# Attention, MoE and gated MLP on one core: cross-partition maxima on TensorE, a list schedule searched over 40 passes, and another way to put float64 weights together

## The chip, the cores and the metric

One Trainium2 chip, one of its cores. The time is that of one execution on the device in microseconds (us), as the median of several runs.

## What is computed

Three stages follow one another on 2304 rows (4 batches of 576 pooled queries, 8 heads of 64):

```python
q_pool = q.reshape(B, H, S // 2, 2, D).mean(axis=3)          # B, H, S, D = 4, 8, 1152, 64
scores = (1 / sqrt(D)) * q_pool @ k.transpose(0, 1, 3, 2)
attn = softmax(scores)                                        # over 1152 keys
x = heads side by side of (attn @ v)                          # 2304 x 512
h = x @ w_in;  x = (h * sigmoid(h)) @ w_out                   # 512 -> 2048 -> 512
out = (((x @ w1) * (x @ w2)) @ w3) @ w_out2                   # 512 -> 1024 -> 1024 -> 512
```

q, k and v are float32. The weights come as float64 and are read as pairs of 32-bit words.

## The kernel before

**Numbers.** Most products use float16 in two parts, a high one and a rest ("hi" and "lo"), each scaled by a power of two that comes from the largest absolute value of the tensor, so that three matmuls (`TERMS`) give nearly float32. Such a scale needs a maximum over all 128 partitions: VectorE (DVE) reduces along the row, `allmax` (L309) then takes the maximum over the partitions on GpSimd (POOL) and gives it to each of them, and `pow2` (L301) makes the scales in a few VectorE instructions on one column.

**Attention.** The work is 144 score tiles of 128 queries x 1152 keys. `tile_ops` (L446) makes, for each: scores on TensorE (PE) into one of two PSUM buffers `sc` (L465), the negative row maximum on VectorE (L502), the exponential with its row sum on ScalarE (ACT, L482), the reciprocal (L487, L490). For batch 0 (`WHOLE`, 36 tiles) the tile is then transposed in float32 on TensorE (L514) and copied out by ScalarE (L517); the reciprocals are spread by `dg` (L523) and a small matmul (`spread`, L562). For the other batches ScalarE and VectorE write a hi and a lo part (L530, L493) and a DMA transposes them (L498). `pv_ops` (L585) multiplies with v (L555 float32, L610 float16); ScalarE writes the result into `x32` (L620). `prep_v` (L386) makes v's two parts for batches 1 to 3, with its maximum (L401, L310).

**First MoE.** Its 9 blocks of 256 rows are made by `block_ops` (L626) and lie between the score tiles on the engines' queues: maximum of `x32` (L632), over partitions (L310), scales (L303 to L638), `x16` hi on ScalarE (L656) and lo on VectorE (L643), then 8 units of `w_in` products (L676), tanh and gate (L692, L695), the hi and lo part of g on ScalarE and GpSimd (L698, L701), 16 units of `w_out` products (L717) and the store.

**Weights.** `from_f64` (L312) makes float32 of the words: ScalarE moves the exponent (L324), then VectorE puts sign, exponent and fraction together in three instructions per 128x512 tile (L328 shifts left by 3, L329 brings in the top three bits of the low word, L330 the sign). There are 72 such tiles: 32 for the first MoE in the first 190 us, 40 for the last stage.

**Last stage.** `w3 @ w_out2` is multiplied out first (L1015), then blocks of 384 rows go through w1 and w2 (L1119), their product (L1139, L1145, L1150) and the final matmul (L1163). Each block's maximum goes over L1087 and L310.

**Order.** Every step is an `op` with an engine, a cost, the buffers that it reads and writes and a key. `Plan.run` (L115) is a list scheduler: engine by engine it takes, among the steps that could start within 0.15 us, the one of least key, and so fixes each engine's order, the order of the DMA issues on SP and which buffer a step gets. Each engine's queue runs in that order; semaphores are waited for in it.

Of the kernel before, what the change touches and what calls it, by code (L numbers as in the profile page):

```python
# [9 lines left out]
F32 = mybir.dt.float32  # L10
F32R = mybir.dt.float32r
F16 = mybir.dt.float16
I32 = mybir.dt.int32
AF = mybir.ActivationFunctionType
# [5 lines left out]
P = 128  # L20
# [7 lines left out]
LOAD_AFTER = 3.0  # L28
AFTER = {PE: 0.25, ACT: 0.2, DVE: 0.15, POOL: 0.2, SP: 0.0}
# [28 lines left out]
class Op:  # L58
    __slots__ = (
        "eng", "cost", "land", "fn", "key", "after", "need", "ready", "start", "end", "takes", "bufs", "n", "hook",  # L60
        "placed",
# [3 lines left out]
class Plan:  # L65
# [5 lines left out]
    def op(self, eng, cost, fn, r=(), w=(), key=0.0, land=None):  # L71
# [3 lines left out]
        o.n, o.hook = len(self.ops), None  # L75
# [39 lines left out]
    def run(self):  # L115
        cand = defaultdict(list)
        free = {e: 0.0 for e in ENGINES}
        free["CTL"] = 0.0
        order = []
# [17 lines left out]
        while any(cand.values()):  # L137
# [11 lines left out]
            assert best is not None, [o.n for some in cand.values() for o in some][:20]  # L149
            at, e, o = best  # L150
            cand[e].remove(o)
            o.start = at
            if e != "CTL":
                free[e] = at + o.cost
            o.end = at + (o.cost if o.land is None else o.land)
# [3 lines left out]
            for buf in o.takes:  # L159
                tag = buf.tag  # L160
                buf.place = min(tag.free, key=lambda s: (tag.free[s], s))
                del tag.free[buf.place]
                tag.next += 1
            for buf in o.bufs:
                buf.left -= 1
                buf.end = max(buf.end, o.end + AFTER.get(e, 0.0))
                if buf.left == 0:
                    buf.tag.free[buf.place] = buf.end
            for x in o.after:
# [15 lines left out]
def kernel(  # L185
# [51 lines left out]
    ident_b = Buf(Tag(1))  # L237

# [24 lines left out]
    t_sm = tags(attn, "sm", 8, [P, 4])  # L263
    t_mv = tags(attn, "mv", 6, [P, 5])
    t_rs = tags(attn, "rs", 1, [P, BL])
    t_dg = tags(attn, "dg", 4, [P, D])
# [42 lines left out]
    def allmax(dst, src):  # L309
        nc.gpsimd.partition_all_reduce(dst, src, channels=P, reduce_op=bass_isa.ReduceOp.max)  # L310

    def from_f64(dst, words, dst_b, words_b, key):  # L312
# [8 lines left out]

        def rebias():
# [9 lines left out]
        op(ACT, 0.68, rebias, [words_b], [dst_b], key)  # L332
        op(DVE, 1.85, merge, [words_b], [dst_b], key + 0.01)
# [13 lines left out]

    kts, qts, v16s, mvs = {}, {}, {}, {}
# [14 lines left out]
    def prep_q(b, g, hp):  # L363
# [20 lines left out]
        op(DVE, 0.7 + 0.13 * g, pool, [qs], [qt], i0 - 7)  # L384

    def prep_v(b, hp):  # L386
        i0 = FIRST_T[(b, 0, hp)]
        v16, mv = attn_buf(t_v16), attn_buf(t_mv) if b >= WHOLE else None
# [10 lines left out]

        def top():  # L400
            nc.vector.reduce_max(mv.t[:, 0:1], vs.t, axis=AX.X, apply_absolute_value=True)  # L401

        def scales():
            pow2(mv.t[:, 1:2], mv.t[:, 2:3], mv.t[:, 3:4])
            nc.vector.tensor_scalar_mul(mv.t[:, 3:4], mv.t[:, 3:4], 2.0 ** 13)
            nc.vector.tensor_scalar_mul(mv.t[:, 4:5], mv.t[:, 2:3], 2.0 ** -29)

        def hi():
            d_, s_ = parts()
            nc.scalar.activation(d_[:, :, 0, :], s_, AF.Copy, scale=mv.t[:, 3:4])  # L410

        def lo():
            d_, s_ = parts()
            nc.vector.scalar_tensor_tensor(
                d_[:, :, 1, :], s_, mv.t[:, 3:4], d_[:, :, 0, :], op0=ALU.mult, op1=ALU.subtract
# [14 lines left out]
        op(DVE, 1.36, top, [vs], [(mv, 0)], i0 - 4)  # L430
        op(POOL, 0.4, lambda: allmax(mv.t[:, 1:2], mv.t[:, 0:1]), [(mv, 0)], [(mv, 1)], i0 - 3.9)
        op(DVE, 0.8, scales, [(mv, 1)], [(mv, 2)], i0 - 2)
        op(ACT, 1.26, hi, [vs, (mv, 2)], [(v16, 0)], i0 - 1)
        op(DVE, 1.45, lo, [vs, (mv, 2), (v16, 0)], [(v16, 1)], i0 + 0.5)

    WHOLE = 1
    pts = {}
    x32s = {}  # L440
    dgs = {}

# [799 lines left out]
```

## Time and profile before

| | |
|---|---|
| median of 3 runs | 1200.62 us (1199.74 to 1205.22) |
| the profiled execution | 1200.74 us, span 1198.7 us |
| mean granted TensorE clock | 0.974 |
| TensorE busy | 1108.2 us (92%) |
| VectorE busy | 792.2 us (66%) |
| ScalarE busy | 663.2 us (55%) |
| GpSimd busy | 158.1 us (13%) |
| 16 DMA engines, hardware queue | 55.6% of the span |

TensorE's busy share is that of a whole span with stages of different limits, and a matmul at the lower clock counts as busy for longer (the nine transposes of one tile took 1.20 us in some places and 2.18 us in others). So the table is only a start: what a stage waits for is read from its own stretch, from the waits that TensorE ends last there, and from the granted clock beside them.

### The profile page before, as it was taken

The numbers are of one execution on the slowest core, as the hardware profiler recorded it, in microseconds if no ns is written. First come the engines' busy times: TensorE is split into PE (matmuls) and PEld (weight loads), VectorE is DVE, ScalarE is ACT, GpSimd is POOL, SyncE is SP. The second block draws the span as 40 slices with busy tenths as digits, with TensorE's granted clock in tenths as the row PEclk, the third lists the DMA queues.
The fourth block names the chain that finished last, engine by engine and source line by source line (L and its number), as shares of the span: only waits on it lengthen the run. The fifth ranks groups of instructions, "written<-read, shape, count | busy, mean of one in ns | idle before, by whom it ended". The sixth has DMA issues, their size and how long they took to land.

```text
span 1198.7 us, 21922 instructions
## 1 busy us (share of the span) xinstructions
PE 1108.2 (92%) x8972; PEld 809.1 (67%) x8972; DVE 792.2 (66%) x1283; ACT 663.2 (55%) x986; POOL 158.1 (13%) x156
## 2 busy tenths in 40 slices
PE   3778897999999999999899999897999999999998
PEld 2445675767776767677677777786756776767666
DVE  6988898498788788797987785576977521212110
ACT  3656667567677577686686675465634322222221
POOL 0000120012012012020020020112121111111211
PEclk9978998999999999999999999898999999999999
DMA  9635344368988997989979778454334001010001
GB/s 348 211 134 184 115 140 157 115 136 169 181 182 171 218 194 166 190 174 200 199 145 200 151 123 148 147 194 137 124 123 150 1 27 54 12 42 27 10 18 27
DMA packets 294821, 163.17 MB, mean 136 GB/s; under 512 B 256064, under 2 KB 266816, under 8 KB 294720
## 3 DMA queue, kind: packets, MB, share of 16 engines
q1 hardware_dynamic: 294720, 161.77, 55.6%
q8 instruction: 70, 1.15, 0.4%
q14 instruction: 31, 0.25, 0.1%
HBM read 80.22 MB, written 9.44 MB: 75 GB/s over the span
## 4 chain that ended last, share of the span: by engine, by line
PE 51%; DVE 3%; issue 2%; DMA 1%; ACT 1%; POOL 1%; DVEq 0%; POOLq 0%; ACTq 0%
PE mt L1119 10%; PE mm L676 7%; PE mt L1163 6%; PE mm L717 5%; PE sc L465 5%; PE mm L1119 4%; PE mm L610 4%; PE mt L1015 3%; PE mt L676 3%; PE mt L717 2%; PE mm L1163 2%; DMA pt<-p 1%; PE mm L1015 0%; DVE sm L502 0%; DVE x L643 0%
## 5 line engine op out<-in xcount | busy, mean ns | idle before, releaser
L465 PE MATMUL sc<-kt,qt 64*128 64x128 f32 (+3 forms) x960 | 200.7, 534 | 29.0 <-ACT pt L517 20.9
L502 DVE TENSOR_REDUCE sm<-sc 128x1 f32<-128x1152 f32 x144 | 193.9, 1348 | 40.5 <-PE sc L465 40.2
L676 PEld LDWEIGHTS <-w 128*128 128x128 f16 x1728 | 169.7, 100 | 60.6 <-issue 35.9
L482 ACT ACTIVATE e<-sc,sm 128x1152 f32<-128x1152 f32 x144 | 175.2, 1217 | 47.9 <-DVE sm L502 42.8
L717 PEld LDWEIGHTS <-w 128*128 128x128 f16 x1728 | 164.3, 98 | 54.2 <-issue 30.9
L676 PE MATMUL mm<-x,w 128*128 128x256 f16 x1440 | 173.2, 279 | 18.6 <-DVE x L643 9.7
L493 DVE SCALAR_TENSOR_TENSOR p<-e,sm,p 128x1152 f16<-128x1152 f32 x108 | 159.5, 1484 | 29.7 <-ACT p L530 29.2
L717 PE MATMUL mm<-g,w 128*128 128x256 f16 x1440 | 169.8, 273 | 2.8 <-POOL g L701 1.9
L465 PEld LDWEIGHTS sc<-kt,qt 64*128 64x128 f32 (+1 forms) x960 | 91.8, 182 | 97.9 <-issue 57.1
L530 ACT ACTIVATE p<-e,sm 128x1152 f16<-128x1152 f32 x108 | 134.2, 1248 | 31.4 <-DMA pt<-p 10.7
L701 POOL TENSOR_TENSOR g<-t,g 128x512 f16<-128x512 f32 x72 | 94.6, 1319 | 297.8 <-ACT g L698 237.0
L1139 DVE SCALAR_TENSOR_TENSOR abf<-mt,x2m,asb 128x384 f32<-128x384 f32 x36 | 22.1, 615 | 123.9 <-PE mt L1119 123.9
L610 PE MATMUL mm<-pt,v 128*64 128x256 f16 (+1 forms) x1944 | 89.8, 250 | 5.3 <-DMA pt<-p 5.1
L610 PEld LDWEIGHTS <-v 128*64 128x64 f16 x1944 | 81.9, 112 | 13.4 <-DMA pt<-p 6.6
L1119 PEld LDWEIGHTS <-w1h 128*128 128x128 f16 x576 | 56.1, 99 | 41.5 <-issue 6.2
L1119 PEld LDWEIGHTS <-w2h 128*128 128x128 f16 x576 | 56.2, 98 | 38.0 <-issue 1.3
L1119 PE MATMUL mt<-x2h,w2h 128*128 128x384 f16 x432 | 76.1, 326 | 0.0
L1119 PE MATMUL mt<-x2h,w1h 128*128 128x384 f16 x384 | 69.4, 331 | 2.1 <-DVE x2h L1081 1.5
L514 PE MATMUL sc<-identr,e 128*128 128x128 f32 x324 | 50.1, 308 | 17.9 <-ACT e L482 17.8
L692 ACT ACTIVATE t<-mm,xm 128x512 f32<-128x512 f32 x60 | 41.1, 685 | 38.4 <-PE mm L676 35.0
L514 PEld LDWEIGHTS sc<-identr,e 128*128 128x128 f32 x324 | 41.1, 158 | 30.1 <-ACT e L482 25.2
L517 ACT COPY pt<-sc 128x1152 f32<-128x1152 f32 x36 | 40.3, 1118 | 32.1 <-PE sc L514 31.9
(131 smaller groups left out, 1336.1 us busy)
## 6 DMA issues: line engine op xcount, KB each, us to landing
v<-in_moe_w_dram SPq DMA_DIRECT2D x32, 512.0 KB, 4.2
qs<-in_q_dram SPq DMA_DIRECT2D x16, 640.0 KB, 4.8
kt<-in_k_dram SPq DMA_DIRECT2D x16, 576.0 KB, 4.6
qs<-in_q_dram SPq DMA_DIRECT2D x16, 512.0 KB, 4.5
g<-in_moe_w_in_dram SPq DMA_DIRECT2D x16, 512.0 KB, 6.1
w<-t SPq DMA_DIRECT2D x32, 256.0 KB, 3.3
stage<-in_v_dram SPq DMA_DIRECT2D x12, 576.0 KB, 4.6
x2d<-t SPq DMA_DIRECT2D x36, 128.0 KB, 2.3
```

Of the source, the lines that this page charges most:

```text
L465: nc.tensor.matmul(sc.t[cols, bank, : (c1 - c0) * P], qt.t[rows * D : (rows + 1) * D, 4 if last else 2 * h + j - 2 * g, cols], kt.t[rows * ...
L482: nc.scalar.activation(e.t, flat(), AF.Exp, bias=sm.t[:, 0:1], accum_out=sm.t[:, 1:2])
L493: nc.vector.scalar_tensor_tensor(p16.t[:, 1], e.t, sm.t[:, 3:4], p16.t[:, 0], op0=ALU.mult, op1=ALU.subtract)
L502: DVE, 1.36, lambda: nc.vector.tensor_reduce(sm.t[:, 0:1], flat(), axis=AX.X, op=ALU.max, negate=True),
L514: nc.tensor.transpose(to[:, c * P : (c + 1) * P], e.t[:, c * P : (c + 1) * P], ident)
L530: ACT, 1.27, lambda: nc.scalar.activation(p16.t[:, 0], e.t, AF.Copy, scale=sm.t[:, 3:4]),
L610: nc.tensor.matmul(ps.t[a * D : (a + 1) * D, :nn], v16.t[:, a, KEYS[c], tv, :], rhs, start=idx == 0, stop=idx == 3 * NK - 1,)
L676: nc.tensor.matmul(ps.t[:, f % 2 * BL : (f % 2 + 1) * BL], w16[0][ct * NQ + f // 4][:, tw, (f % 4) * P : (f % 4 + 1) * P], x16.t[:, ct, tx ...
L701: nc.gpsimd.tensor_tensor(gv(1), two(g32), gv(0), op=ALU.subtract)
L717: nc.tensor.matmul(ps.t[:, :BL], w16[1][f][:, tw, ct * P : (ct + 1) * P], gs[u].t[:, f % 4, tg, :], start=f == 0 and n == 0, stop=f == NF ...
L1119: nc.tensor.matmul(ps.t[:, :TB], buf.t[:, ct, tw, f * P : (f + 1) * P], xr.t[:, ct, tx, :], start=idx == 0, stop=idx == 11,)
L1163: nc.tensor.matmul(ps.t, ab[f].t[:, ta, m * P : (m + 1) * P], w3_b.t[:, f, tb, :], start=f == 0 and n == 0, stop=f == NF2 - 1 and n == 2,)
```

## The change

- `allmax` is gone. `top_mm` takes its place at all 24 places: a float32 matmul with the identity as moving operand and the column, broadcast to 128 columns, as stationary one, which puts the 128 values of the column side by side on every partition in PSUM, then a VectorE maximum along the row.
- For blocks 2 to 7 (batches 1 to 3) the scale of x no longer comes from x. It comes from the maximum of |v| of the batch (`vmx`), which bounds the attention's output; it is made when the last v of the batch is prepared. Where the block's results come late (all of the second block of a batch, the last quarter of the first), ScalarE and VectorE write `x16` straight from PSUM, without `x32`.
- `from_f64` now has two VectorE instructions. GpSimd takes the top three bits of the low word's upper byte (`top3`), ahead of them.
- `spread` reads the reciprocals straight, broadcast, so the `dg` tiles (L523) are gone.
- `Plan.run` builds the schedule 40 times from keys that are moved at random towards each step's latest start, and takes the one with the earliest end by its own costs. A change of `mode` on TensorE costs 0.1 us in it, some costs are altered, scores keep their order, and a score tile follows the transpose three tiles earlier.

```diff
     def run(self):
...
+        some = random.Random(1)
+        best, keys = None, None
+        for n in range(ROUNDS):
...
+            order = self.go()
+            if order is not None:
+                end = max(o.end for o in order)
+                if best is None or end < best[0]:
+                    best = end, [(o, o.start, o.end) for o in order], [(b, b.place) for b in bufs]
+                    keys = [o.key for o in self.ops], self.late(order, end)
+            part, noise = some.random(), 6.0 * some.random() ** 2
+            for o, key, last in zip(self.ops, keys[0], keys[1]):
+                o.key = key + part * (last - key) + noise * some.gauss(0.0, 1.0)
...
-    def allmax(dst, src):
-        nc.gpsimd.partition_all_reduce(dst, src, channels=P, reduce_op=bass_isa.ReduceOp.max)
+    def top_mm(dst, src, r, w, key):
+
+        am = Buf(t_mm)
+        op(
+            PE, 0.3,
+            lambda: nc.tensor.matmul(am.t[:, :P], src().to_broadcast([P, P]), ident, start=True, stop=True),
+            [r], [am], key,
+        )
+        op(DVE, 0.22, lambda: nc.vector.reduce_max(dst(), am.t[:, :P], axis=AX.X), [am], [w], key)
...
+        def top3():
+            lo = words()[:, :, 0]
+            nc.gpsimd.tensor_scalar(
+                lo, words().bitcast(U8)[:, :, 3], 2.0 ** -5, -31.0 / 64.0, op0=ALU.mult, op1=ALU.add
+            )
...
-            nc.vector.tensor_scalar(di, di, 3, None, op0=ALU.logical_shift_left)
-            nc.vector.scalar_tensor_tensor(di, lo, 29, di, op0=ALU.logical_shift_right, op1=ALU.bitwise_or)
+            nc.vector.scalar_tensor_tensor(di, di, 3, lo, op0=ALU.logical_shift_left, op1=ALU.bitwise_or)
             nc.vector.scalar_tensor_tensor(di, hi, SIGN, di, op0=ALU.bitwise_and, op1=ALU.bitwise_or)
...
-        op(POOL, 0.4, lambda: allmax(mv.t[:, 1:2], mv.t[:, 0:1]), [(mv, 0)], [(mv, 1)], i0 - 3.9)
+        top_mm(lambda: col(1), lambda: col(0), (mv, (hp, 0)), (mv, (hp, 1)), i0 - 3.9)
...
+        if straight:
+
+            def x_hi():
+                nc.scalar.activation(x16.t[:, hp, 0], ps.t[:, :nn], AF.Copy, scale=mv.t[:, 5, hp : hp + 1])
+
+            def x_lo():
+                nc.vector.scalar_tensor_tensor(
+                    x16.t[:, hp, 1], ps.t[:, :nn], mv.t[:, 5, hp : hp + 1], x16.t[:, hp, 0],
+                    op0=ALU.mult, op1=ALU.subtract,
+                )
...
-        op(DVE, 1.25, top, [x32], [(xm, 0)], i - 6)
-        op(POOL, 0.4, lambda: allmax(xm.t[:, 1:2], xm.t[:, 0:1]), [(xm, 0)], [(xm, 1)], i - 6)
...
+        if not (bound and g):
+            got = [(x32, (h_, 0)) for h_ in range(n_)] if bound else [x32]
+            to = [[(x16, (h_, t)) for h_ in range(n_)] for t in range(2)]
+            op(ACT, 0.15 + 0.25 * n_, hi, got + [(xm, 2)], to[0], i - 6)
+            op(DVE, 0.15 + 0.27 * n_, lo, got + [(xm, 2)] + to[0], to[1], i - 6)
```

Three places show what moves. The first is GpSimd's queue at the start of the last stage, before the change: `g` are the parts of the gated product, `ws` the maximum of w1 and w2, `x2m` that of a block; a row `ISA` without operands sets GpSimd up for another kind of instruction.

```order
L701 TENSOR_TENSOR g_178<-t_0_184,g_178 128x2x256
L310 ISA
L310 ISA ws_192<-ws_192 128x1
L701 ISA
L701 TENSOR_TENSOR g_178<-t_2_186,g_178 128x2x256
L701 TENSOR_TENSOR g_179<-t_1_185,g_179 128x2x256
L701 TENSOR_TENSOR g_179<-t_0_184,g_179 128x2x256
L701 TENSOR_TENSOR g_180<-t_4_188,g_180 128x2x256
L701 TENSOR_TENSOR g_180<-t_1_185,g_180 128x2x256
L310 ISA
L310 ISA x2m_8626<-x2m_8626 128x1
L1150 ISA
```

The same place now (L823 is the old L701; L388 is `top3`, on the words `v` of the last stage's weights):

```order
L388 TENSOR_SCALAR v_3_7820<-v_3_7820 128x512
L823 TENSOR_TENSOR g_176<-t_2_183,g_176 128x2x256
L388 TENSOR_SCALAR v_0_7817<-v_0_7817 128x512
L388 TENSOR_SCALAR v_1_7818<-v_1_7818 128x512
L388 TENSOR_SCALAR v_2_7819<-v_2_7819 128x512
L823 TENSOR_TENSOR g_177<-t_4_185,g_177 128x2x256
L388 TENSOR_SCALAR v_3_7820<-v_3_7820 128x512
L823 TENSOR_TENSOR g_177<-t_2_183,g_177 128x2x256
L823 TENSOR_TENSOR g_174<-t_0_181,g_174 128x2x256
```

The all-reduces and the `ISA` rows are gone from the whole queue but for its start and end (73 `ISA` rows before, 3 now); `top3` lies between the g parts.

The second place is VectorE's queue at the start of block 5 of the first MoE, before (`x_0_115` is `x32`, `x_0_181` the block's `x16`, `sc` and `p` belong to score tiles):

```order
L632 TENSOR_REDUCE xm_191<-x_0_115 128x1
L493 SCALAR_TENSOR_TENSOR p_1_110<-e_107,sm_122,p_1_110 128x1152
L303 TENSOR_SCALAR xm_191<-xm_191 128x1
L304 TENSOR_SCALAR xm_191<-xm_191 128x1
L307 TENSOR_SCALAR xm_191<-xm_191 128x1
L637 TENSOR_SCALAR xm_191<-xm_191 128x1
L638 TENSOR_SCALAR xm_191<-xm_191,wst_72 128x1
L502 TENSOR_REDUCE sm_124<-sc_81 128x1
L643 SCALAR_TENSOR_TENSOR x_0_181<-x_0_115,xm_191,x_0_181 128x4x256
```

And now (L610 is the old L502, L596 the old L493, `mm_84` the product with v in PSUM):

```order
L610 TENSOR_REDUCE sm_121<-sc_81 128x1
L610 TENSOR_REDUCE sm_120<-sc_82 128x1
L596 SCALAR_TENSOR_TENSOR p_1_111<-e_108,sm_119,p_1_111 128x1152
L730 SCALAR_TENSOR_TENSOR x_1_179<-mm_84,mv_131,x_1_179 128x256
L590 TENSOR_SCALAR sm_121<-sm_121 128x1
```

One instruction on 256 columns is left of the block's own chain on VectorE.

The third place is TensorE's queue in batch 0, around the maximum of `w_in` (L568 are scores, L622 transposes, L371 is the matmul of `top_mm`):

```order
L568 MATMUL sc_82<-kt_102,qt_98 128x512 x2
L568 MATMUL sc_82<-kt_102,qt_98 128x128
L568 MATMUL sc_81<-kt_102,qt_98 128x512 x2
L568 MATMUL sc_81<-kt_102,qt_98 128x128
L622 MATMUL sc_82<-identr,e_109 128x128 x9
L371 MATMUL mm_83<-identr,wst_72 128x128
L568 MATMUL sc_82<-kt_99,qt_97 128x128
```

Where GpSimd stood aside with such a maximum before, TensorE's own queue now holds it, and the score tiles behind it start after it. Over the whole queue the 144 score tiles lie in 114 unbroken runs instead of 134; behind batch 0's last transpose it is 83 instead of 98. 17 of the 24 `top_mm` matmuls stand ahead of the last score tile, 5 of them in batch 0.

## Rows read from the trace of the kernel before

**Rows 1.** Busy time of each engine in six stages; start:end, length, busy.

```profile
core 0: us, PE busy (x) PEld busy (x) DVE busy (x) ACT busy (x) POOL busy (x), PEclk, DMA share, GB/s
0.00:240.00 240.00, 190.98 (x1367) 129.56 (x1368) 193.61 (x382) 146.65 (x210) 13.64 (x21) 0.92 0.51 176
240.00:735.00 495.00, 477.02 (x4803) 357.98 (x4802) 408.05 (x600) 352.63 (x485) 71.69 (x62) 0.99 0.88 173
735.00:765.00 30.00, 23.40 (x298) 19.37 (x291) 12.15 (x22) 9.43 (x14) 0.73 (x2) 0.89 0.70 135
765.00:860.00 95.00, 85.29 (x758) 74.64 (x756) 72.06 (x110) 60.70 (x118) 20.53 (x18) 0.96 0.47 153
860.00:905.00 45.00, 42.23 (x233) 25.91 (x231) 35.08 (x56) 19.09 (x34) 9.50 (x9) 0.96 0.43 138
905.00:1199.00 294.00, 289.32 (x1530) 201.61 (x1528) 71.28 (x116) 74.69 (x128) 42.04 (x44) 1.00 0.11 36
```

**Rows 2.** What TensorE waited for: us in total, times, longest.

```profile
PE sc L465 <- ACT pt L517: 20.9, 17, 2.0
PE sc L514 <- ACT e L482: 17.8, 8, 7.0
PE mm L676 <- DVE x L643: 9.7, 8, 1.9
PE mt L717 <- POOL g L701: 9.6, 2, 8.9
PE mm L676 <- ACT x L656: 8.2, 6, 3.5
```

**Rows 3.** Two groups of VectorE that go: busy us, mean ns.

```profile
L328 DVE TENSOR_SCALAR w<-w 128x512 int32<-128x512 int32 x48 | 21.0, 438 | 6.3 <-ACT w L324 6.2
L523 DVE TENSOR_SCALAR dg<-identr,sm 128x64 f32<-128x64 f32 x36 | 8.7, 249 | 5.7 <-PE mm L562 5.5
```

**Rows 4.** L329: ns min/median/max; then the longest, and GpSimd beside it.

```profile
L329 DVE SCALAR_TENSOR_TENSOR w<-w,w x8: 691/693/1702, 75.2 to 180.0; 128x512 int32<-128x512 int32 x8
...
156.72 1.70 DVE L329 SCALAR_TENSOR_TENSOR w<-w,w 128x512 int32<-128x512 int32 x1
...
156.72 1.15 POOL L701 TENSOR_TENSOR g<-t,g 128x512 f16<-128x512 f32 x1 [7.54 <-ACT v L410]
```

**Rows 5.** Timeline 754 to 761 us: start, length, what, idle before it.

```profile
754.27 0.47 ACT L620 ACTIVATE x<-mm,mv 128x256 f32<-128x256 f32 x1 [6.40 <-PE mm L610]
754.77 1.22 DVE L632 TENSOR_REDUCE xm<-x 128x1 f32<-128x1024 f32 x1 [8.67 <-ACT x L620]
756.13 0.38 POOL L310 PARTITION_ALL_REDUCE xm<-xm  x1 [43.55 <-DVE xm L632]
...
758.91 0.27 PE L676 MATMUL mm<-x,w 128*128 128x256 f16 x1 [3.53 <-ACT x L656]
...
760.23 2.08 PE L676 MATMUL mm<-x,w 128*128 128x256 f16 x9 [1.05 <-DVE x L643]
```

**Rows 6.** Timeline 820 to 836 us, GpSimd and TensorE.

```profile
826.18 0.38 POOL L310 PARTITION_ALL_REDUCE ws<-ws  x1 [6.15 <-issue]
...
834.59 3.38 POOL L701 TENSOR_TENSOR g<-t,g 128x512 f16<-128x512 f32 x3 [8.04 <-issue]
...
835.79 5.76 PE L717 MATMUL mt<-g,w 128*128 128x256 f16 x36 [8.89 <-POOL g L701]
```

**Rows 7.** Transposes of batch 0; two and one score tile in the chain.

```profile
L514 PE MATMUL sc<-identr,e 128*128 128x128 f32 x324 | 50.1, 308 | 17.9 <-ACT e L482 17.8
...
557.42 2.15 PE sc L465 x10
...
575.39 1.27 PE sc L465 x5
```

**Rows 8.** Timeline 892 to 897 us: second block of the last stage.

```profile
892.08 0.38 POOL L310 PARTITION_ALL_REDUCE x2m<-x2m  x1 [7.08 <-issue]
...
896.60 3.52 PE L1119 MATMUL mt<-x2h,w1h 128*128 128x384 f16 x11 [1.53 <-DVE x2h L1081]
```

More of the change, by code (lines that the diff above doesn't have):

```diff
@@ L1 @@
 import math
+import random
 from collections import defaultdict
@@ L115, in run, with late, go @@
     def run(self):
+        bufs = {id(b): b for o in self.ops for b in o.bufs}.values()
+        tags = {id(b.tag): b.tag for b in bufs}.values()
+        ops = [(o, o.need, o.ready) for o in self.ops]
+        left = [(b, b.left) for b in bufs]
+        free = [(t, dict(t.free)) for t in tags]
+        some = random.Random(1)
+        best, keys = None, None
+        for n in range(ROUNDS):
+            for o, need, ready in ops:
+                o.need, o.ready, o.frees = need, ready, []
+            for b, n_ in left:
+                b.left, b.end, b.place, b.users = n_, 0.0, None, []
+            for t, f in free:
+                t.free, t.next, t.last = dict(f), 0, {}
+            order = self.go()
[7 more added lines that the diff above has]
+                o.key = key + part * (last - key) + noise * some.gauss(0.0, 1.0)
+        for b, place in best[2]:
+            b.place = place
+        for o, start, stop in best[1]:
+            o.start, o.end = start, stop
+        return [o for o, _, _ in best[1]]
+    def late(self, order, end):
+        first = {}
+        for o in sorted(order, key=lambda o: (-o.start, -o.n)):
+            last = end
+            gap = AFTER.get(o.eng, 0.0)
+            for x in o.after:
+                last = min(last, first[x] - (0.0 if x.eng == o.eng and o.land is None else gap))
+            for x in o.frees:
+                last = min(last, first[x] - gap - (LOAD_AFTER if x.eng == SP else 0.0))
+            first[o] = min([last - o.end + o.start] + [first[x] for x in o.placed])
+        return [first[o] for o in self.ops]
+    def go(self):
         cand = defaultdict(list)
@@ L148, in run @@
                     best = at, e, o
-            assert best is not None, [o.n for some in cand.values() for o in some][:20]
+            if best is None:
+                return None
             at, e, o = best
@@ L152, in run @@
             o.start = at
+            late = 0.0
+            if e == PE and o.mode != mode:
+                late, mode = SWITCH, o.mode
             if e != "CTL":
-                free[e] = at + o.cost
-            o.end = at + (o.cost if o.land is None else o.land)
+                free[e] = at + o.cost + late
+            o.end = at + (o.cost if o.land is None else o.land) + late
             order.append(o)
@@ L162, in run @@
                 del tag.free[buf.place]
+                for x in tag.last.get(buf.place, ()):
+                    x.frees.append(o)
                 tag.next += 1
@@ L168, in run @@
                     buf.tag.free[buf.place] = buf.end
+                    buf.tag.last[buf.place] = buf.users
             for x in o.after:
@@ L441 @@
     dgs = {}
+    turns, asked = {}, {}
     def pt32(pt):
@@ L570, in pv_whole @@
         sp, rs = Buf(t_mm), attn_buf(t_rs)
-        op(
-            PE, 0.3 if last else 0.6, spread, [ident_b] + [dg for k_, dg in inv.items() if not last or k_ == (0, 0)],
+        first = op(
+            PE, 0.3 if last else 0.6, spread, [ident_b] + [(dg, 2) for k_, dg in inv.items() if not last or k_ == (0, 0)],
             [sp, (rs, 0)], i + 1.0,
@@ L575, in pv_whole @@
         op(ACT, 0.3 if last else 0.45, lambda: nc.scalar.copy(rs.t[:, :nn], sp.t[:, :nn]), [sp], [(rs, 1)], i - SOON)
-        op(PE, 1.4 if last else 4.5, pv, [v16] + list(mine.values()), [ps, (x32, (hp, off, 0))], i + 2.5)
+        pv_op = op(PE, 1.1 if last else 4.4, pv, [v16] + list(mine.values()), [ps, (x32, (hp, off, 0))], i + 2.5, mode=2)
+        plan.link(pv_op, {first})
         op(
@@ L591, in pv_ops @@
         blk = 2 * B if last else 2 * b + g
-        if blk not in x32s:
+        straight = b >= WHOLE and not last and (g == 1 or hp == NP - 1)
+        if straight:
+            x16 = x16s[blk]
+        elif blk not in x32s:
             x32s[blk] = attn_buf(t_x32t if last else t_x32)
-        x32 = x32s[blk]
+        x32 = None if straight else x32s[blk]
         off = b * TAIL if last else 0
```

192 lines of the change are left out of this document (121 added, 71 removed).

## The prediction

> **What bounds the kernel now.** I read the busy time by stage first, then TensorE's own waits, then VectorE's groups and the places in the timeline that the waits point to. In the stages the reader should subtract TensorE's busy time from the length and look at the clock beside it [rows 1]. From 240 to 735 us TensorE is busy for 477.0 of 495 us, and from 905 us on for 289.3 of 294: there TensorE's work is the time. Its idle time lies elsewhere: 49.0 us in the first 240, 18.0 in the next stage, 6.6 around the end of attention (735 to 765), 9.7 until 860, 2.8 until 905, 4.7 behind that; in all 90.8 us. The clock comes on top. A mean below 1 is a mix of its two levels, 2.4 and 1.2 GHz, and busy time times the missing share is what it cost: 191.0 x 0.08 = 15 us in the first stage, 5 in the second, about 3, 3 and 2 in the next three, 28 in all. It falls where TensorE had stood idle just before. So some 119 us are at stake at most, of which the first matmul's 7 us and the 4.7 at the end stay.
>
> Who ends the waits: ScalarE's copy and exponential of the batch-0 tiles (20.9 and 17.8 us), the two parts of x16 at a block's start (9.7 and 8.2 us), and GpSimd's part of g (9.6 us, of them 8.9 in one piece) [rows 2]. The first pair belongs to a loop through VectorE, which is busy for 193.6 of 240 us in that stage (81%) [rows 1], while a score tile has only two PSUM buffers.
>
> **The sum, part by part.** The profiled execution took 1200.74 us, 0.1 above the median of the runs shown, so I sum against 1200.7.
>
> *First 240 us.* VectorE loses one instruction for each of 32 weight tiles (438 ns) and 36 `dg` tiles (249 ns) [rows 3]: 14.0 + 9.0 = 23.0 us. GpSimd's `top3` is new and has no row. Its length lies between next to nothing and the 1.15 us of a two-input subtract on 512 columns. What it costs VectorE I bound by what such a subtract did to the same kind of instruction: 1.70 us instead of 0.69, so 0 to 1.01 us each [rows 4]. That is dear only when VectorE issues an instruction with two SBUF tensors while `top3` is under way. The two that are left to a tile, at 0.69 us, hold 44 of the stage's 193.6 us, nearly a quarter; I take a fifth of the dear end, since others of the kind come beside them but many meet `top3` only in part: 0.2 us, 6.4 for 32 tiles. With 1.5 us for the row maxima of the new matmuls VectorE is left with 15 us less. At a busy share of 0.81 that shortens the stage by 15 / 0.81 = **19 us**, the clock that comes back with it included. Ends: +13 (at 1.01 us a tile VectorE has (32 - 23 + 1.5) / 0.81 = 13 us more) and -40 (nearly all idle time behind the first matmul).
>
> The rule that speaks against this step: by the Trainium skill (SBUF — State Buffer, "Who interferes with whom") a VectorE instruction with two SBUF inputs and a GpSimd instruction that reads SBUF exclude each other for the whole instruction, and the one that was issued second waits. The 1.70 us agrees [rows 4]; by the rule at its worst, every `top3` in front of such an instruction, this stage would come out at the +13 end instead of -19.
>
> *Blocks of the first MoE, 240 to 735 us.* A block's start costs TensorE its wait for x16. The chain in one such place: copy out of PSUM 0.47 us from 754.27, maximum 1.22 us, GpSimd, scales, hi part, and the last wait ends at 760.23, 6.0 us behind the copy's start [rows 5]. For blocks 2 to 7 the copy becomes the hi part and one VectorE instruction on 256 columns follows (an estimate of 0.45 us, after the copy of as many): 1 us instead of 6, and the scale is known long before. Of the 17.9 us of waits [rows 2], 4.6 belong to 758.9 and 760.2 us [rows 5]; of the other 13.3 I take **-9**, since blocks 0 and 1 keep their chain, and **-2** for the clock behind the longer ones. Ends: 0 (another wait, such as a late DMA transpose, stands at the same place) and -18 (all idle time of the stage).
>
> Merging runs of score tiles: two together take 2.15 us, one alone 1.27 [rows 7], so a run less saves 0.39 us; 15 runs less behind batch 0 are **-6** (0 if the work between them pays for its own switches, -6 at best). The 24 new matmuls have no row; the nearest is a float32 transpose of the same 128 columns, 308 ns [rows 7], with 0.35 us as I take it: 12 in this stage, **+4**; 7 behind attention, **+2**. Those in batch 0 lie in idle time and cost nothing; if that idle time is gone they are 2 us, counted above. Sum of the stage: -9 - 2 - 6 + 4 = **-13**.
>
> *End of attention, 735 to 765 us.* The same chain for blocks 7 and 8 together, behind the last product with v, with nothing else for TensorE: 3.53 + 1.05 us of waits [rows 5] and 3 us of clock. **-6** (0 to -9).
>
> *765 to 860 us.* GpSimd's all-reduce and its ordinary instructions need different set-ups, and here each change made it stand 6 to 8 us without a releaser: 6.15 us in front of the all-reduce, 8.04 in front of the next subtracts, and TensorE waited 8.89 us for their result [rows 6]. With no all-reduce in the queue there is no change of set-up: -9, and -2 of the clock behind it, **-11** (-5, if VectorE's weight tiles are what is late next, to -13). VectorE loses 40 more 438 ns instructions, 17.5 us, here and until 960; most of it is no gain, since TensorE has work of its own there, and it covers the 40 `top3`: 8 us at 0.2, 40 at worst.
>
> *860 to 905 us.* The second block's scale waits in the same way for GpSimd (7.08 us of set-up) and TensorE 1.53 us for x2h [rows 8], more for its first part, and lower clock: **-3** (0 to -4). Behind 905 us nothing but the +2 above.
>
> Sum: 1200.7 - 19 - 13 - 6 - 11 - 3 + 2 = 1150.7, so **1151 us**. The passes of the scheduler have no term of their own: they are made on its own costs, and what I count is work and chains that go.
>
> **Rivals.**
>
> *The passes pay as well.* If the order found closes most of what is left (idle time and clock were 119; mine leaves about 70), say all but 12 us of fixed ends, 20 in batch 0 and 14 elsewhere, the time is 1200.7 - 119 + 46 = 1128. For it: 49 us of idle time in a stage whose VectorE is only 81% busy [rows 1]. Against: the scheduler's costs know neither port nor clock.
>
> *The maxima hold up TensorE's queue.* Each `top_mm` matmul stands in order; where its column is late on VectorE, the score tiles and products behind it wait too, which GpSimd's queue did not make them do. At the mean of the waits for VectorE's part of x16, 9.7 / 8 = 1.2 us [rows 2], 24 of them give back 29 us: 1180. Against: in the order they stand behind other work, not right behind their reduction.
>
> *Slower: `top3` paces VectorE.* If `top3` takes 1.4 us and VectorE waits for the whole of it, each costs 1.2 us more than I took. A microsecond of it costs 32 / 0.81 = 40 us in the first stage and, at half weight, some 15 behind 765 us: 55 x 1.2 = 66, so 1217. The change turns at 0.2 + 50 / 55 = 1.1 us of wait a tile. For it: that VectorE instruction that lost 1.01 us [rows 4]; against: it is the longest of its group, whose median is 0.693.
>
> *No change.* The set-up time stays although the all-reduce goes: `top3` and the subtract alternate 39 times in GpSimd's queue. At 6 us [rows 6] for even a third of these in front of something that TensorE needs, that is 13 x 6 = 78 us, of which a good half shows: the 50 us gone, about 1200. Against: every such wait in the trace stands next to an all-reduce, and the order has no set-up row between the two.
>
> **How the numbers follow.** Forecast and its neighbours from 1134 to 1170: 0.54. The passes pay as well (below 1134): 0.14. The maxima hold up the queue (1170 to 1194): 0.17. No change that can be measured, within 0.5% or 6 us: 0.06. Slower than that: 0.09. So faster is 0.85. The range goes from 1124, a little under the first rival, to 1188, most of the second: about two in ten lie outside. The port's bounds are in it from 0 to 0.85 us a tile.
>
> **What would show it.** Right: no set-up waits of 6 to 8 us on GpSimd and no wait of TensorE for g around the end of the first MoE; waits for x16 at the blocks' starts of 5 us in all rather than 17.9; TensorE's idle time in batch 0 near 30 us rather than 49, and the last transpose of batch 0 some 19 us earlier. Wrong: L398 and L399 with medians well over 0.69 us, `top3` rows over 1.2 us, or TensorE idle in front of L371. If the gain is there but lies in batch 0 beyond 25 us, it is the order and not the work taken away that made it.

## The result and the profile after

The changed kernel takes **1141.96 us** (median of 4 runs, 1139.54 to 1143.81), the kernel before 1202.19 on the same chip (1199.74 to 1205.22): a ratio of 0.9497 (95% interval 0.9464 to 0.953), 60 us less. The prediction said 1151, with a range of 1124 to 1188. The profiled execution has a span of 1137.8 us against 1198.7.

To see where the 60.9 us between the spans came from, I cut both traces at the same events of TensorE rather than at the same times: the start of the last transpose of batch 0, of the last score matmul, of the last product with v, and of the first product with w1 (`x2h`). Lengths in us:

| stretch | before | after | difference |
|---|---|---|---|
| to the last transpose of batch 0 | 236.5 | 213.8 | -22.7 |
| to the last score matmul | 499.0 | 476.5 | -22.5 |
| to the last product with v | 19.7 | 20.2 | +0.5 |
| to the first product with w1 | 102.0 | 86.0 | -16.0 |
| to the end | 341.5 | 341.3 | -0.2 |

The cut is kind to the fourth row: after the change, TensorE waits for x2h for 3.0 us right behind that first product, and the wait falls into the last row. Counted with it, the stretch up to w1 gains 13 us.

Busy time after, cut at these events (columns as in [rows 1]):

```profile
0.00:213.80 213.80, 182.19 (x1358) 127.72 (x1359) 176.51 (x310) 143.24 (x207) 34.57 (x46) 0.91 0.55 194
213.80:690.30 476.50, 472.56 (x4824) 362.08 (x4823) 404.84 (x626) 349.48 (x482) 67.70 (x48) 1.00 0.91 182
690.30:710.50 20.20, 18.44 (x286) 16.48 (x282) 6.62 (x12) 8.04 (x12) 0.00 (x0) 1.00 0.92 156
710.50:796.50 86.00, 85.01 (x786) 75.80 (x779) 73.94 (x94) 56.76 (x111) 47.75 (x46) 1.00 0.62 201
```

TensorE's idle time in the whole span is 1137.8 - 1091.7 = 46 us where it was 90.5. What is left is two thirds in batch 0 (31.6 us); the stretch of the blocks has 3.9 us, the one up to w1 1.0, the last 7.8.

The mean clock of batch 0 is 0.92 before and 0.91 after, but the two can't be compared. The clock records of the trace before begin at 40.0 us, and a window without a record prints as 1.00. The transposes in it show the lower level, 1.2 GHz: a tile's nine take 2.18 us there and 1.20 behind it.

```profile
0.00:40.00 40.00, 19.98 (x64) 12.00 (x65) 28.00 (x52) 15.92 (x22) 0.69 (x6) 1.00 0.84 301
26.13 2.18 PE L514 MATMUL sc<-identr,e 128*128 128x128 f32 x9 [7.00 <-ACT e L482]
47.51 1.20 PE L514 MATMUL sc<-identr,e 128*128 128x128 f32 x9
```

After the change the records begin at 10.2 us, with the upper level, and the first tile takes 1.20:

```profile
11.99 1.20 PE L622 MATMUL sc<-identr,e 128*128 128x128 f32 x9 [1.35 <-ACT e L585]
```

If the time ahead of the first record counts as the lower level in both, the means of the stage are 0.84 and 0.89 (an estimate from these records).

What TensorE waits for, after:

```profile
PE sc L568 <- ACT pt L625: 10.4, 11, 2.1
PE sc L622 <- ACT e L585: 8.5, 6, 3.2
PE sc L568 <- DMA kt<-in_k_dram: 6.3, 1, 6.3
...
PE mm L1254 <- DVE x2h L1216: 3.0, 1, 3.0
...
PE mm L371 <- DVE wst L889: 0.6, 1, 0.6
PE mm L371 <- DVE t L817: 0.5, 1, 0.5
...
PE mt L839 <- POOL g L823: 0.4, 1, 0.4
```

The first two are those of [rows 2] and have halved (20.9 and 17.8 us). The 17.9 us for the two parts of x16 and the 9.6 us for g are down to fractions of a microsecond, and the matmul of `top_mm` (L371) itself waits for 1.1 us in all.

GpSimd's waits without a releaser, before:

```profile
POOL g L701 <- issue: 46.0, 8, 8.0
POOL x2m L310 <- issue: 24.7, 4, 7.1
POOL abr L1150 <- issue: 7.1, 1, 7.1
POOL ws L310 <- issue: 6.2, 1, 6.2
POOL mv L310 <- issue: 6.1, 1, 6.1
```

and after:

```profile
POOL g L823 <- issue: 1.0, 1, 1.0
```

13 waits of 5.8 to 8.0 us, 87 us together, are gone (two of g's eight were short, 1.4 and 1.6 us). The rows of the new instructions, as ns min/median/max and the times of the first and the last: `top3` (L388), of the last stage's weights and of the first ones:

```profile
L388 POOL TENSOR_SCALAR v<-v x40: 653/976/1134, 717.6 to 846.8; 128x512 int32<-128x512 uint8 x40
L388 POOL TENSOR_SCALAR g<-g x16: 642/659/1252, 7.6 to 53.8; 128x512 int32<-128x512 uint8 x16
```

the second merge behind it on VectorE (L399), of the first weights and of the last stage's:

```profile
L399 DVE SCALAR_TENSOR_TENSOR w<-g,w x16: 691/693/1083, 12.7 to 78.7; 128x512 int32<-128x512 int32 x16
L399 DVE SCALAR_TENSOR_TENSOR w<-v,w x16: 692/1036/1532, 719.0 to 758.7; 128x512 int32<-128x512 int32 x16
```

and the matmul and the reduction of `top_mm` for v:

```profile
L371 PE MATMUL mm<-identr,mv x24: 275/275/377, 129.9 to 585.1; 128*128 128x128 f32 x24
L374 DVE TENSOR_REDUCE mv<-mm x12: 272/284/291, 131.4 to 585.5; 128x1 f32<-128x128 f32 x12
```

In the first 150 us `top3` takes 0.66 us and the merge its 0.69; for the weights of the last stage the medians are 0.98 and, for the 16 merges shown, 1.04 (0.85 for the other 24). A maximum stands as two matmul rows in the trace (24 for 12), 0.39 us from the start of the first to the end of the second where nothing holds them up.

### The profile page after: what moved, and what is told of

It reads as the page before. It is cut to its first block, busy times and chain, and to the rows that moved or that the text cites. A ratio compares the mean times of both kernels' runs of the same rounds, so it can differ in the third digit from the quotient of the medians.

```text
span 1137.8 us, 21941 instructions
## 1 busy us (share of the span) xinstructions
PE 1091.7 (96%) x9020; PEld 811.2 (71%) x9020; DVE 764.4 (67%) x1194; ACT 657.2 (58%) x983; POOL 211.8 (19%) x198
## 4 chain that ended last, share of the span: by engine, by line
PE 77%; DVE 6%; DMA 3%; issue 2%; ACT 2%; SPq 0%; POOL 0%; DVEq 0%; ACTq 0%; POOLq 0%
PE mt L1254 12%; PE sc L568 12%; PE mm L798 12%; PE mm L839 12%; PE mm L715 7%; PE mt L1298 6%; PE mm L1254 4%; PE mt L1150 3%; PE mm L1298 2%; DMA pt<-p 2%; PE mt L798 1%; PE sc L622 1%; PE mm L656 1%; DVE sm L610 1%; DVE t L817 1%
## 5 line engine op out<-in xcount | busy, mean ns | idle before, releaser
L610 DVE TENSOR_REDUCE sm<-sc 128x1 f32<-128x1152 f32 x144 | 192.7, 1351 | 32.3 <-PE sc L568 30.2
L568 PE MATMUL sc<-kt,qt 64*128 64x128 f32 (+3 forms) x960 | 193.6, 525 | 20.3 <-ACT pt L625 10.4
L823 POOL TENSOR_TENSOR g<-t,g 128x512 f16<-128x512 f32 x72 | 100.3, 1398 | 528.9 <-ACT g L820 515.5
L839 PEld LDWEIGHTS <-w 128*128 128x128 f16 x1728 | 165.6, 98 | 35.7 <-issue 13.4
L839 PE MATMUL mm<-g,w 128*128 128x256 f16 x1488 | 173.3, 273 | 1.9 <-DMA w<-t 1.5
L798 PE MATMUL mm<-x,w 128*128 128x256 f16 x1440 | 168.1, 275 | 1.2 <-DVE t L817 0.4
L596 DVE SCALAR_TENSOR_TENSOR p<-e,sm,p 128x1152 f16<-128x1152 f32 x108 | 155.4, 1453 | 13.6 <-ACT p L631 13.1
L568 PEld LDWEIGHTS sc<-kt,qt 64*128 64x128 f32 (+1 forms) x960 | 92.1, 181 | 86.8 <-issue 55.9
L1254 PE MATMUL mt<-x2h,w1h 128*128 128x384 f16 x444 | 76.8, 326 | 0.0
L1254 PE MATMUL mt<-x2h,w2h 128*128 128x384 f16 x420 | 72.5, 326 | 0.0
L622 PE MATMUL sc<-identr,e 128*128 128x128 f32 x324 | 48.4, 305 | 8.5 <-ACT e L585 8.5
L814 ACT ACTIVATE t<-mm,xm 128x512 f32<-128x512 f32 x60 | 41.0, 684 | 23.1 <-PE mm L798 20.2
L622 PEld LDWEIGHTS sc<-identr,e 128*128 128x128 f32 x324 | 40.6, 156 | 19.1 <-ACT e L585 13.5
```

The costliest lines, as they stand in the source:

```text
L568: nc.tensor.matmul(sc.t[cols, bank, : (c1 - c0) * P], qt.t[rows * D : (rows + 1) * D, 4 if last else 2 * h + j - 2 * g, cols], kt.t[rows * ...
L596: nc.vector.scalar_tensor_tensor(p16.t[:, 1], e.t, sm.t[:, 3:4], p16.t[:, 0], op0=ALU.mult, op1=ALU.subtract)
L610: DVE, 1.36, lambda: nc.vector.tensor_reduce(sm.t[:, 0:1], flat(), axis=AX.X, op=ALU.max, negate=True),
L622: nc.tensor.transpose(to[:, c * P : (c + 1) * P], e.t[:, c * P : (c + 1) * P], ident)
L798: nc.tensor.matmul(ps.t[:, f % 2 * BL : (f % 2 + 1) * BL], w16[0][ct * NQ + f // 4][:, tw, (f % 4) * P : (f % 4 + 1) * P], x16.t[:, ct, tx ...
L823: nc.gpsimd.tensor_tensor(gv(1), two(g32), gv(0), op=ALU.subtract)
```

## The experiments

My theory (**work**) was the prediction's: the time comes from work and chains that go (VectorE's instructions, the blocks' chains, GpSimd's set-up). The rival (**search**) was that the 40 passes make it; a third (**port**) that `top3` gives back on VectorE what it saves. Each ratio is to the kernel before, timed beside it on the same chip; in brackets its 95% interval. Where two figures stand for a difference between two kernels, one is by their medians, the other by their ratios (times 1202 us). The diffs are against the changed kernel unless "before" is named.

**One pass only.**

```diff
-ROUNDS = 40
+ROUNDS = 1
```

> The changed kernel with one pass of the scheduler instead of 40 (new costs, links and work all kept). If the gain comes from work and chains that were taken away, as the prediction summed it, the passes are worth at most 10 us and this takes 1142 to 1152 us. If the search made the gain, most of the 60 us go back: 1175 us or more.

Measured: 1156.9 us, 0.9592 [0.9559, 0.9625]. Neither theory's band. Without any search the changed program is 45 to 49 us faster than the one before; the passes are worth another 11 to 15 (in the profiled spans 15: 9.3 in batch 0, 10.8 in the stretch of the blocks, some back around the end of attention).

**The passes on the program before.** The scheduler's new classes in the kernel before, everything else as it was.

> The kernel before with the new scheduler alone: 40 passes, and the cost of a change of mode, which no step of this kernel has. Work, costs and chains are the old ones. If work and chains made the gain, this is 1185 to 1202 us. If the search did, it is 1165 us or less, most of the way to 1142.

Measured: 1183.4 us, 0.9817 [0.9772, 0.9863]. The passes alone give 19 to 22 us there. So with the passes on both sides the other parts are worth 38 to 41 us, without them 45 to 49.

**Another seed.**

```diff
-        some = random.Random(1)
+        some = random.Random(2)
```

> The changed kernel with another seed for the random part of the passes (2 instead of 1); costs, code and the number of passes are the same. If the some 15 us between one pass and 40 come from searching as such, another 40 passes find an order about as good: 1137 to 1148 us. If 1142 was the luck of one seed, this comes out where one pass did, at 1152 to 1160, and the prediction's sum without a term for the passes was the better account.

Measured: 1136.65 us, 0.9429 [0.9386, 0.9471]. So the gain of the passes isn't one seed's luck; this version is 5 to 8 us ahead of the change, though the two intervals just meet. TensorE's idle time is 48 us against 46, its busy time 5.7 us less, with a higher clock in batch 0 (0.97 against 0.91).

**300 passes.**

```diff
-ROUNDS = 40
+ROUNDS = 300
```

> The changed kernel with 300 passes instead of 40, same seed, nothing else. If searching goes on paying (1 pass 1157, 40 passes 1142, another 40 passes with another seed 1137), 300 find another 4 to 12 us: 1130 to 1138. If what the scheduler still finds lies below what its own costs can tell (they know no port and no clock), the time stays within the spread of two seeds: 1137 to 1146.

Measured: 1141.95 us, 0.9506 [0.9467, 0.9545]: nothing beyond the 40. By the scheduler's costs a later pass can only be as good or better; the chip doesn't follow it any more.

**Three VectorE instructions again, no `top3`,** in the changed kernel's order:

```diff
-            nc.vector.scalar_tensor_tensor(di, di, 3, lo, op0=ALU.logical_shift_left, op1=ALU.bitwise_or)
+            nc.vector.tensor_scalar(di, di, 3, None, op0=ALU.logical_shift_left)
+            nc.vector.scalar_tensor_tensor(di, lo, 29, di, op0=ALU.logical_shift_right, op1=ALU.bitwise_or)
```

> The changed kernel in its very order, but the weights are put together in three VectorE instructions again and GpSimd's step for the top bits does nothing. VectorE gets 72 x 0.44 us more and is rid of the waits for GpSimd. If a third of a hit is the price of top3 (0.2 us), VectorE has 0.24 us a tile too much, 8 us in the first 215 us: 1148 to 1154 us. If top3 holds VectorE up for as long as it saves, the time stays within 3 us of 1142, and if it paces VectorE it falls to 1135 or less.

Measured: 1152.3 us, 0.9561 [0.9526, 0.9596], 8 to 10 us more than the change. The last transpose of batch 0 starts at 221.5 instead of 213.8: 7.7 us.

**No `top3`,** same order, two merges:

```diff
-            lo = words()[:, :, 0]
-            nc.gpsimd.tensor_scalar(
-                lo, words().bitcast(U8)[:, :, 3], 2.0 ** -5, -31.0 / 64.0, op0=ALU.mult, op1=ALU.add
-            )
+            return None
...
-            _, di, lo, hi = parts()
+            _, di, _, hi = parts()
+            lo = zero.bitcast(I32).to_broadcast([P, di.shape[1]])
```

> The changed kernel in the same order, but GpSimd's top3 issues nothing and VectorE's first merge takes a column of zeros instead of the low word: the low three bits of every weight are left out. VectorE's two instructions stay as they are. By the prediction's price (0.2 us of VectorE for each of 32 tiles, over a busy share of 0.81, and up to 8 us behind attention) the time falls by 5 to 14 us: 1128 to 1137. By the trace's means (0.15 us a tile over the first 32, 0.48 over the last 40) by 4 to 12. Rival: top3 costs the path nothing: 1140 to 1144.

Measured: 1137.0 us, 0.9435 [0.9385, 0.9486]: 5 to 7 us less, at the edge of what the intervals tell apart. But the rows are plain. The late merges have their old length back:

```profile
L399 DVE SCALAR_TENSOR_TENSOR w<-v,w x16: 691/692/1606, 720.5 to 757.0; 128x512 int32<-128x512 int32 x16
```

against a median of 1036 above, and VectorE is busy for 749.3 us instead of 764.4. That is 15.1 / 72 = 0.21 us a tile, but not the same everywhere: in batch 0 it is 3.4 us (176.5 against 173.1), 0.11 us for each of its 32 tiles.

**`top3` twice,** same order:

```diff
+            nc.gpsimd.tensor_scalar(
+                lo, words().bitcast(U8)[:, :, 3], 2.0 ** -5, -31.0 / 64.0, op0=ALU.mult, op1=ALU.add
+            )
```

> The changed kernel in the same order with top3 issued twice for each weight tile (the second one finds the low word already rewritten, so that the low three bits are lost). At the prediction's price the second 72 cost what the first do: 5 to 14 us, so 1147 to 1156. If VectorE must wait for the whole of each (0.65 to 0.98 us; the rival in which top3 sets VectorE's pace), the first 32 alone cost 26 to 39 us: 1168 or more. If GpSimd's work lies wholly aside: 1140 to 1144.

Measured: 1158.15 us, 0.9601 [0.9557, 0.9645]: 12 to 16 us more, the median 2 above the band for the prediction's price and well short of the one in which VectorE waits for each `top3`. But they do not fall where I had put them. The last transpose of batch 0 starts at 214.5 instead of 213.8, so 32 more `top3` cost that stage 0.7 us, though VectorE is busy for 4.9 us more in it (181.4 against 176.5). The stretch from the last product with v to w1 is 14.8 us longer, and two waits of TensorE there are not for VectorE:

```profile
PE mm L842 <- POOL g L826: 5.9, 1, 5.9
PE mt L842 <- POOL g L826: 5.4, 1, 5.4
```

`top3` stands in front of g's lo part in GpSimd's own queue. In this order that is the dear side of it, not the port.

**All-reduces back, in the order planned without them.** The matmul's place in TensorE's order stays empty, the reduction on VectorE is an all-reduce on GpSimd instead.

> The changed kernel in its very order, but each maximum over partitions is GpSimd's all-reduce again, in place of the VectorE maximum behind the matmul (TensorE's step does nothing, so TensorE has 24 x 0.3 us less). If the set-up of GpSimd for two kinds of instructions was worth its term, waits of 6 to 8 us come back at most of the 24 places and top3 and the subtracts stand behind them: 1157 us or more, with TensorE waiting for GpSimd's part of g. If the shorter chains and not the set-up gave the gain, it stays within 5 us of 1142.

Measured: 1181.6 us, 0.9797 [0.9762, 0.9831], 36 to 40 us more. The last transpose of batch 0 starts 19.0 us later, the stretch of the blocks takes 8.5 more, w1's first product comes another 14 behind the last product with v, and GpSimd has 18 waits of 5.8 to 8.1 us without a releaser again.

**All-reduces back, planned again.**

```diff
-        am = Buf(t_mm)
         op(
-            PE, 0.3,
-            lambda: nc.tensor.matmul(am.t[:, :P], src().to_broadcast([P, P]), ident, start=True, stop=True),
-            [r], [am], key,
+            POOL, 0.4,
+            lambda: nc.gpsimd.partition_all_reduce(dst(), src(), channels=P, reduce_op=bass_isa.ReduceOp.max),
+            [r], [w], key,
         )
-        op(DVE, 0.22, lambda: nc.vector.reduce_max(dst(), am.t[:, :P], axis=AX.X), [am], [w], key)
```

> The changed kernel with every maximum over partitions again by GpSimd's all-reduce, and planned again in 40 passes with the all-reduce at the 0.4 us that the scheduler before gave it (the earlier run put it into an order planned without it and took 40 us more). If set-up time on GpSimd is the price wherever the all-reduce stands, it costs this order much the same, since the passes do not know of it: 25 to 45 us, 1167 to 1187. If a good part of the 40 us was an order that had no room for it, what is left are the 14 us of the prediction's two terms, less 6 us of matmuls that go: 8 to 15 us, 1150 to 1157. If the maxima on TensorE paid nothing at all, as they did alone in the kernel before: 1137 to 1146.

Measured: 1164.1 us, 0.9675 [0.9631, 0.972], 22 us more: between the two bands. So about half of the 40 was an order that had no room for them. Batch 0 is 8 us shorter and the stretch of the blocks 12 longer; most of what is left lies in the stretch from the last product with v to w1, 109.0 us instead of 86.0. The timeline there, GpSimd first:

```profile
802.41 0.98 POOL L386 TENSOR_SCALAR v<-v 128x512 int32<-128x512 uint8 x1
809.26 0.38 POOL L370 PARTITION_ALL_REDUCE x2m<-x2m  x1 [5.88 <-PE mt L837]
816.96 1.85 POOL L386 TENSOR_SCALAR v<-v 128x512 int32<-128x512 uint8 x2 [7.33 <-issue]
```

and TensorE:

```profile
794.55 15.12 PE L837 MATMUL mt<-g,w 128*128 128x256 f16 x137 [1.33 <-POOL g L821]
821.52 0.48 PE L1252 MATMUL mt<-x2h,w1h 128*128 128x384 f16 x1 [11.85 <-ACT x2h L1234]
```

`top3` sits on both sides of the all-reduce. GpSimd stands for 5.88 us ahead of it and 7.33 behind it, x2h comes after it, and TensorE is idle for 11.85 us where the change has 3.0.

**The maxima alone, on the kernel before,** in one pass: `allmax` replaced by `top_mm` at its five calls, which make 30 maxima there (the change has 24, since its blocks 2 to 7 have none of their own).

> The kernel before, planned by its own scheduler in one pass, with one part of the change alone: every maximum over partitions by a matmul against the identity and a reduction on VectorE instead of GpSimd's all-reduce; no bound from v, no merged runs of scores, weights as before. By the prediction's terms this takes away the set-up waits, 11 + 3 us, and adds 12 x 0.35 + 2 us of matmuls: 8 us less, 0.990 to 0.996 of the time before. The rival, from the run in which the all-reduces came back into the new order for 40 us: the all-reduce was dearer than the waits that I could see, and this part alone gives 20 to 40 us: 0.967 to 0.983. If the matmuls hold up TensorE's queue: above 1.0.

Measured: 1210.9 us, 1.0067 [1.0041, 1.0094]: a little slower. Batch 0 (-6.5 us), the end of attention (-3.8) and the stretch to w1 (-4.6) gain, but the stretch of the blocks is 28 us longer. Part of that is work that stands in it now and stood elsewhere before (155 more matmul rows, 28 of them the new maxima's own); part is a bad place of the new order, where score tiles follow each other with nothing between:

```profile
510.00:530.00 20.00, 13.27 (x49) 6.49 (x48) 18.58 (x29) 14.26 (x19) 0.00 (x0) 0.63 0.68 184
```

That is TensorE idle for 6.7 us, every wait for an exponential, and a mean clock of 0.63, so most of these 20 us at 1.2 GHz. TensorE stands 5.6 us in front of the new matmuls in the whole span: the rival that named them is right in the sign, but not as the main cause.

**The weights alone, on the kernel before,** in one pass: `from_f64` as in the change.

> The kernel before, planned by its own scheduler in one pass, with the weights put together by top3 on GpSimd and two VectorE instructions, nothing else. By the prediction's terms VectorE loses 32 x 0.44 us and gets 32 x 0.2 back before 240 us: 7.6 / 0.81 = 9 us less, 0.991 to 0.994 of the time before. The rival: with the all-reduces still in GpSimd's queue, top3 stands behind their set-up waits of 6 to 8 us and the weights come late, or VectorE waits for the port: no gain or slower, 0.998 to 1.02. More than 0.985 would say that VectorE's instruction was worth more than its length.

Measured: 1210.45 us, 1.0073 [1.0049, 1.0098]: slower, as the rival said. VectorE's busy time in batch 0 falls from 192.9 to 186.2 us, near the 7.6 worked out, and yet the stage is 7.5 us longer. The timeline of one place shows why, GpSimd first, then VectorE and TensorE:

```profile
116.73 0.63 POOL L325 TENSOR_SCALAR x<-x 128x512 int32<-128x512 uint8 x1 [7.23 <-issue]
123.43 0.38 POOL L311 PARTITION_ALL_REDUCE mv<-mv  x1 [6.07 <-issue]
...
124.18 0.15 DVE L304 TENSOR_SCALAR xm<-xm 128x1 f32<-128x1 f32 x1 [10.38 <-POOL xm L311]
...
127.57 2.42 PE L472 MATMUL sc<-kt,qt 64*64 64x128 f32 x12 [10.78 <-ACT pt L524]
```

`top3` put among the all-reduces makes GpSimd change its set-up more often: nine times in the first 245 us instead of five, four of them as waits without a releaser (28 us), where the kernel before has none such in this stage. One of them stops VectorE for 10.38 us and TensorE for 10.78.

**The blocks' own maxima,** planned again:

```diff
-        straight = b >= WHOLE and not last and (g == 1 or hp == NP - 1)
+        straight = False
...
-        bound = WHOLE <= b < B
+        bound = False
...
-        xms[blk] = xms[blk - 1] if blk % 2 and blk >= 2 * WHOLE else moe_buf(t_xm)
+        xms[blk] = moe_buf(t_xm)
```

and without the three steps in `prep_v` that made scales from `vmx`.

> The changed kernel, planned again, in which blocks 2 to 7 and the tail block keep their own chain as before: copy of the product with v, maximum over x, the matmul for the maximum over partitions, scales, high and low part; the bound from v is left out (but for the tail block, which keeps it). By the prediction's terms this gives back 9 + 2 us of waits for x16 and clock between 240 and 735 us, and most of the 6 us around the end of attention: 1153 to 1160. Rival: a list schedule in 40 passes lays other work beside the chains, and they are worth little: 1142 to 1147. A third case, above 1162, would say that the bound was worth more than its waits.

Measured: 1165.8 us, 0.9663 [0.9616, 0.971]: 20 to 24 us more, the median beyond the upper case. TensorE idles 18.6 us more in all, about 7 in batch 0, 7 in the blocks and the rest around w1's start. In the stretch of the blocks its waits come in many small pieces, first of all:

```profile
PE mm L707 <- DMA pt<-p: 3.3, 2, 2.9
PE mm L790 <- DVE t L809: 2.8, 2, 2.2
PE sc L560 <- ACT e L577: 1.5, 2, 1.2
PE mm L790 <- DVE x L754: 1.0, 1, 1.0
```

Only a part of them is for x16 (L790 for x). The chain's instructions on ScalarE and VectorE make other steps late too.

## Why the prediction came right, point by point

**Direction, range and the four places** are as forecast. Set-up waits and the wait for g are gone, x16 costs under 1 us instead of 17.9, and each of the three stages that were to gain did, by 22.7, 22.5 and 16 us. That two of them came out well above their terms is not the terms' doing: with one pass, which is what the sum counted, the four stretches up to w1 are 13.4, 11.7, 3.6 and 15.5 us shorter than before, and the whole span 46. So the 50 us of the sum are about what the work gave; its split over the stages fits less well.

**Batch 0: -22.7, forecast -19.** The size fits by luck, the working only in part: 13.4 us come from the work, 9.3 from the passes. VectorE's terms were near: `top3` costs it 0.11 us a tile here, taken as 0.2, and the third instruction put back costs 7.7 us where (14.0 - 6.4) / 0.81 makes 9.4. The clock's cost was read too small, since the 0.92 leaves out the first 40 us. And the exchange by the busy share holds only while nothing else paces the stage. With `top3` twice nothing came of it (0.7 us), and with the all-reduces kept it had the wrong sign. My rival on set-up asked whether `top3` and the subtract change it; they don't. That the weights' part needs the maxima's part, because `top3` and the all-reduce do, I hadn't seen.

**Blocks: -22.5, forecast -13.** The step at fault is "of the other 13.3 I take -9": the chains were priced by TensorE's waits for x16 alone. Taking them back costs 20 to 24 us over the whole kernel, spread over several stages; about 16 of it stand in the blocks, where some is work that moved there. Merged runs of scores, the clock, the `dg` tiles and the scheduler's altered costs and earlier transposes were not tried by themselves.

**Up to w1: -16.0 (and +0.5), forecast -6 and -11.** Bringing the all-reduce back, planned again, costs 23 us in just this stretch, more than the 14 that I had for set-up; `top3` is now beside it. But the set-up isn't the whole account. On the kernel before, with all 30 all-reduces kept and no `top3`, the 40 passes alone bring this stretch from 102.0 to 91.3 us and TensorE's idle time in it from 14.3 to 4.3 us. In that order both maxima stand behind the last subtract, with one change of set-up, and TensorE waits for no g:

```profile
825.35 1.34 POOL L756 TENSOR_TENSOR g<-t,g 128x512 f16<-128x512 f32 x1 [2.62 <-ACT g L753]
833.48 0.38 POOL L365 PARTITION_ALL_REDUCE ws<-ws  x1 [6.79 <-issue]
833.77 0.42 POOL L365 PARTITION_ALL_REDUCE x2m<-x2m  x1
```

So a better place for the all-reduces gives most of this term as well; the 23 us are their price in a queue that has `top3`.

**The last stage: -0.2, forecast -1.** Two small terms that cancel, neither tried alone.

**The passes.** "The passes of the scheduler have no term of their own" is the sentence that failed. They are worth 11 to 15 us on the changed program and 19 to 22 on the one before. With one pass the change takes 1156.9, so without them the forecast was 6 us too low; with them, 9 too high. The first rival had the right kind of gain and too much of it, 1128. Why they help, though the costs know neither port nor clock, I can't say from these runs beyond where: in batch 0 and the blocks of the changed program, in batch 0 (8.5 us) and up to w1 (10.7) of the one before. One thing goes with it: the traces of three of the four one-pass orders (before, one pass, the maxima alone) have no clock record ahead of 40 us, those of the searched orders begin at 10 to 19. Each kernel has one trace, so whether the order does it stays open. 300 passes gave no more; that the costs can't tell any more is an argument, not shown.

**The port.** By the Trainium skill (SBUF — State Buffer, "Who interferes with whom") a VectorE instruction with two SBUF inputs and a GpSimd instruction that reads SBUF shut each other out. The rows agree: a median of 1.04 us for the late merge, 0.692 when `top3` is taken away. Of the 144 merge instructions after the change, 45 took more than 0.85 us, and each of these began while a GpSimd instruction was under way; of the other 99 only four did. By my own sign (L399 well over 0.69 us) the price of `top3` was too low for the last 40 tiles: VectorE is busy for 11.6 us less behind the last score matmul without it, 0.29 us a tile. It cost the kernel 5 to 7 us in all. At the rule's worst case the stage would have lost 13 us instead of winning; it didn't, since in batch 0 the two seldom met (0.693 in the median).

**The maxima's price.** Taken as 0.35 us each on TensorE, 0.39 in the trace. By the Trainium skill (GPSIMD Engine Reference, "4.1 Engine selection") a reduction along partitions belongs on GpSimd. For a column of 128 values this case says otherwise: two matmul rows and a 0.28 us reduction replace a 0.38 us all-reduce with 6 to 8 us around it, and with `top3` in the same queue the kernel is 22 us faster for it where both are planned in 40 passes. Without `top3`, in one pass, it gained nothing.

## What to carry over

Two edits that share an engine can each be worth nothing alone and much together: the maxima and the weights each made the kernel before 8 us slower, in the one order tried, and taking either back out of the change costs 22 and 8 to 10 us. (No run has just these two, and such prices overlap: they don't add up.) Before pricing an instruction that goes to GpSimd, look what kind stands next to it in that queue, and count the changes of kind. A chain's worth isn't the sum of the waits that name it, since its instructions also stand in front of others. And where a change plans the order anew, some 10 to 20 us of 1200 are the order's own; undo a part with the planner run again as well as in the fixed order, and believe the difference only where both agree.

## What the runs showed of the hardware

- Between an all-reduce and an ordinary instruction GpSimd stood for at least 5.74 us, in both directions and at every one of the 40 changes in the trace before, not only the first; at the 146 changes in the four other kernels with all-reduces it was at least 5.8. Of these, 13 were waits without a releaser before (87 us) and 21 with `top3` added (141 us). A long wait without a releaser alone is no proof: three kernels without any all-reduce have one or two of 5.8 to 8.3 us between two subtracts.
- A float32 matmul of 128x128 against the identity is recorded as two rows of 0.275 us, where a float32 transpose of as much is one of 0.273.
- The printed mean clock counts the time ahead of a trace's first clock record as full speed: in the trace before, 1.00 for the first 40 us, in which a tile's transposes took 2.18 us.
- `top3` reads every eighth byte of its tile, 512 bytes a partition, and took 0.64 to 0.66 us where it ran undisturbed; in the crowded stage 0.98.
